# Natural keys taken from the products of A, 40-column stationaries, a scheduler that counts instruction transfers, and 128-row products for y

## The chip, the cores and the metric

The kernel runs on one core of a Trainium2 chip. The metric is the device time of one execution in microseconds (us); less is better. The engines are TensorE (PE, with its weight loader PEld), VectorE (DVE), ScalarE (ACT), GpSimd (POOL) and SyncE (SP, which here only issues DMAs).

## The reference, cut to what matters

A recurrence over 768 steps for 4 x 8 heads of 40 x 40 state, and a gated feed-forward block on its output:

```python
for t in range(S):
    y[:, :, t] = einsum('bhd,bhde->bhe', rt, state)
    Sa = einsum('bhde,bhe->bhd', state, at)
    state = state * wt[:, :, None, :] - einsum('bhd,bhe->bhde', Sa, bt)
    state = state + einsum('bhd,bhe->bhde', vt, kt)
xn = x / sqrt(mean(x * x) + 1e-6) * rms_g      # x: 3072 x 320
g = xn @ w_gate;  val = xn @ w_val             # 320 x 1536, stored as float64
out = (g * sigmoid(g) * val) @ w_out           # 1536 x 320
```

## The kernel before, in words

**Tiling.** The recurrence is cut into 24 chunks of C = 32 steps; all 32 heads are worked at once, as 8 groups n of (i, o) pairs: i is the upper or lower 64 partitions where the steps of k and b (or v and U) lie, o which head of the pair. LEVELS = 1, 2, 4, 8, 16 are the steps of a doubling scheme inside a chunk.

**`front(c)`** (L467) needs only the inputs. It loads w and a (`wan`), k and b (`kbn`), v (`VU`) and every second w (`wn`), turns them on PE (`turned`, 8 transposes of 128x128 against `ident`), and then for each level l multiplies K and A (32 products, "A,K", L502), puts the result under a mask into LT (`where`, DVE), and scales K and A for the next level (DVE and ACT copies). `natural` (L456) turns K back so that its steps lie on partitions (`KN[l]`): 8 transposes and a copy, for l = 4, 8, 16 and 32, so four K transposes a chunk. LT goes through DRAM (`sB`) into M, one row of 32 x 32 per head.

**`inverse(c)`** (L537) solves M by 31 pairs of small DVE operations on `Yi` and sends the result back through `sY` into LT.

**`main(c)`** (L558) is the recurrence over chunks: X (ST,aP and VU,LT), U (Xs,LT), the state update "up" (VU,KN), the scores sc (rE,vut), their masked copies As (one per level, DVE, L609), y's base (rE,Sd and r,Sd, L638) and five `level` products (As,KN, L616: 32 products of 64 rows x 64 stationary columns, 16 moving columns). Of the 64 stationary columns 24 are not needed (the next head's, or padding). Then y is turned (`xn`), squared on ACT (`sq`, with a sum), raised to -1/2 on POOL, scaled on ACT to x, turned again ("ident,x", L666) and scaled to `xg`.

**`feed(g)`** (L671) works on two chunks: for 12 blocks f of 128 columns of the feed-forward, 4 products on 128 rows and 2 on 64 rows (inputs 256 to 319) in one batch (L685), Silu (ACT), a product (DVE) and 2 output products (L690). Weights come from `sW` in DRAM into five buffers `wf`. `narrow` (L701), 24 calls, first converts them from float64 there, through the buffers wf, sg and hT that the feed uses too.

**What sets the order.** Nothing is issued when it is written. `plan.add` takes each piece with an engine, a due time and a cost; `Plan.issue` (L118) then runs a simulation and writes the program in the order that comes out. Each engine takes, of the pieces that are ready, the one due first. For PE it also models a clock that halves after a 3.41 us window with few columns (ENOUGH, KEEP, L47) and prefers wide pieces then, and it puts fillers (`warm`, L740: a 128x128 product that nobody reads) into PE's idle time until the first feed product. SP's and ACT's DMA issues are pieces too; `swapped` (L451) issues k, b and v on ACT's queue, all other loads are on SP's.

Of the kernel before, what the change touches and what calls it, by code (L numbers as in the profile page):

```python
# [22 lines left out]
N0, NF = 60.0, 6.0  # L23
S0, S1 = 36.0, 8.0
LAG = 10.0
EPS = 1e-6


class Piece:


    def __init__(self, engine, due, time, issue, lane=0.0, columns=0, paced=False, room=None, since=0.0):
        self.engine, self.due, self.time, self.issue = engine, due, time, issue
        self.lane, self.columns, self.paced, self.room = lane, columns, paced, room
        self.ready, self.missing, self.users = since, 0, []


class Plan:
# [6 lines left out]
    LATENCY, SELF = 0.18, 0.115  # L45
    SWITCH, STICK = 0.1, 4.0
    WINDOW, ENOUGH, KEEP = 3.41, 1600, 1300  # L47
    LOOK, LOW = 1.0, 1300
    AHEAD, FAR = 0.0, 20.0
    WARM = 200.0  # L50
# [67 lines left out]
    def issue(self):  # L118
# [5 lines left out]
        clock, columns, recent, lane, order, full, fed = [0.5], {}, [], 0.0, [], False, False  # L124

        def put(i):
            p = P_[i]
            (held if p.paced and p.due > pace + self.FAR else waiting[p.engine]).append(i)

# [7 lines left out]
        for _ in P_:  # L137
            t, e = min((max(free[e], min(at_least(i) for i in w)), e) for e, w in waiting.items() if w)
            can = [i for i in waiting[e] if at_least(i) <= t]
            if e == "PE":  # L140
                since = max(free[e], 3.0)
                while not fed and t < self.WARM and since + 0.3 < t:
                    w = int(since / self.WINDOW)
                    while len(clock) <= w:
                        c = columns.get(len(clock) - 1, 0)
                        clock.append(1.0 if c >= (self.ENOUGH if clock[-1] < 1 else self.KEEP) else 0.5)
                    order.append((since, None))
                    columns[w] = columns.get(w, 0) + 256
                    since += 0.214 / clock[w]
                at = int(t / self.WINDOW)  # L150
                while len(clock) <= at:
                    c = columns.get(len(clock) - 1, 0)
                    clock.append(1.0 if c >= (self.ENOUGH if clock[-1] < 1 else self.KEEP) else 0.5)
# [3 lines left out]
                many = [i for i in can if P_[i].columns >= 500]  # L157
                if many and (clock[at] < 1 or had < self.LOW):
# [3 lines left out]
            i = min(can, key=lambda i: (P_[i].due + (self.STICK if e == "PE" and (P_[i].columns > 0) != full else 0), i))  # L162
# [3 lines left out]
            if e == "PE":  # L166
                end = t + (p.time + (self.SWITCH if (p.columns > 0) != full else 0)) / clock[at]
                full, fed = p.columns > 0, fed or p.paced is True
# [5 lines left out]
            if p.lane:  # L174
                lane = max(lane, end + 1.2) + p.lane
                end = lane + 0.7
# [9 lines left out]
            for j in p.users:  # L186
                u = P_[j]
                u.ready = max(u.ready, end + (self.LATENCY if u.engine != e else 0 if e == "PE" else self.SELF))
                u.missing -= 1
                if not u.missing:  # L190
                    put(j)
# [19 lines left out]
def kernel(  # L211
# [122 lines left out]
    def mm(o, lhsT, rhs, start=True, stop=True):  # L334
        return o, lhsT, rhs, lambda at: nc.tensor.matmul(at(o), lhsT, rhs, start=start, stop=stop, skip_group_check=True)  # L335

    def flip(o, i, ident):
        return o, i, ident, lambda at: nc.tensor.transpose(at(o), i, ident)  # L338

    def pe(due, time, steps, columns=0, paced=False, more=[]):  # L340
        def issue(at):
            for s in steps:
                s[3](at)
        plan.add("PE", due, time + 0.02, issue, [s[0] for s in steps] + more, [x for s in steps for x in s[1:3]],
                 columns=columns, paced=paced)
# [5 lines left out]
                            compare_op=ALU.not_equal, fill=1.0)  # L351

# [6 lines left out]
    for j, l in enumerate(LEVELS):  # L359
        nc.vector.tensor_scalar(iw[:, 2], iw[:, 0], j, None, ALU.logical_shift_right)  # L360
        nc.vector.tensor_scalar(msk[:, j], iw[:, 2], 1.0, None, ALU.is_equal)
    mhalf = const.tile([P, 1], FP32, name="mhalf")
# [31 lines left out]
    tail = lambda t: t[:, NI * D:]  # L394
# [4 lines left out]
    VU_ = Turns(2, [P, N, 2, 64], "VU", whole)  # L399
    ST_ = Turns(2, [P, N, 2, 64], "ST", whole)  # L400
    LT_ = Turns(3, [P, NI, C], "LT", whole)
    KN_ = {l: Turns(3, [P, NI * D + 24], f"KN{l}_", tail) for l in LEVELS[1:] + (32,)}
    Sd_ = Turns(2, [P, NI * D + 24], "Sd", whole)
    T_ = Turns(3, [P, NI * 63], "T")
    K_ = Turns(3, [P, NI, 2, C], "K")
    A_ = Turns(3, [P, NI, C], "A")
    aP_ = Turns(2, [P, NI, C], "aP")
    M_ = Turns(1, [P, C, C], "M")
# [7 lines left out]
    As_ = Turns(1, [P, len(LEVELS), NI, 16], "As")  # L416
# [11 lines left out]
    po_ = psum.tile([P, 2, 512], FP32, name="po")  # L428
# [13 lines left out]
    def turned(due, t, paced=False):  # L442

        ps = plan.room().rearrange("p u f -> p (u f)").rearrange("p (n t) -> p n t", n=N)
        pe(due, 0.95, [flip(ps[:, n, :], t[:, n].rearrange("p o e -> p (o e)"), ident) for n in range(N)], 1024, paced)
# [5 lines left out]
    def swapped(due, t, i, x, src, tk):  # L451

        for q in range(2):
            dma(due, flat(t)[rows(i, x ^ q), q * H:(q + 1) * H, 0:D], src[2 * i + q, :, tk, :].rearrange("h s d -> s h d"), "ACT")

    def natural(due, l, K):  # L456
        ps = turned(due, K.rearrange("p (n i) x s -> p n i (x s)", i=2))
        t = KN_[l].next()
        copy(due, t[:, 0:NI * D].rearrange("p (n o e) -> p n o e", n=N, o=2),
             ps.rearrange("p n (o e) -> p n o e", o=2)[:, :, :, 0:D])  # L460
        return t

    def kn(z, l, i, n, o):
        w_ = D if l > 1 else 64
        return z["KN"][l][half(i), (2 * n + o) * w_:(2 * n + o) * w_ + 64]

    def front(c):  # L467
# [5 lines left out]
        for i in range(2):  # L473
# [6 lines left out]
            for x in range(2):  # L480
                at = i * 64 + x * C
                dma(d - T, wn[at:at + C:2], w[2 * i:2 * i + 2, :, c * C + 1:(c + 1) * C:2, :].rearrange("q h s d -> s (q h) d"))
        ps = turned(d + 4.2, wa).rearrange("p n (i x t) -> p (n i) x t", i=2, x=2)
# [6 lines left out]
        copy(d + 7.2, Tl[1], ps[:, :, 0, :])  # L490
        A = A_.next()
        copy(d - 0.9, A, ps[:, :, 1, :])
        K = K_.next()
        copy(d + 2, K.rearrange("p (n i) x s -> p n (i x s)", n=N), turned(d + 2, kb))
        LT = z["LT"] = LT_.next()
        z["KN"] = {1: flat(kb).rearrange("p a e -> p (a e)"), 2: KN_[2].next()}
        tt(d + 1.3, z["KN"][2][:, 0:NI * D].rearrange("p (a e) -> p a e", e=D), flat(kb)[:, :, 0:D], wn, MUL)
        for j, l in enumerate(LEVELS):
            G = C // (2 * l)
            due = d + 5 + 7.5 * j  # L500
            gr = plan.room().rearrange("p o (n t) -> p o n t", n=N)[:, :, :, 0:16]
            pe(due - 0.7, 0.95, [mm(gr[half(i), o, n, :], K[part(o), 2 * n + i].rearrange("p x s -> p (x s)"),  # L502
                              side(A, l, 1)[part(o), 2 * n + i]) for n, i, o in each])
            where(due, side(LT, l, 1), side(msk, l, 1)[:, j:j + 1].bitcast(U32).to_broadcast((P, NI, G, l)),
                  gr.rearrange("p o n t -> p (o n) t").rearrange("p n (g l) -> p n g l", g=G))
            if l > 2:
                z["KN"][l] = natural(due + 2, l, K)
# [4 lines left out]
            if G == 1 or l == 1:  # L512
                lr = lambda t: t.rearrange("p n x (g h l) -> p n x h (g l)", h=2, l=l)
                tt(due + 0.1, lr(K1)[:, :, :, 0], lr(K)[:, :, :, 0], t[:, :, None, :, 1].to_broadcast((P, NI, 2, 16)), MUL)
            else:
                for x in range(2):
                    tt(due + 1.6, side(K1[:, :, x], l, 0), side(K[:, :, x], l, 0), by[1], MUL)
            for x in range(2):
                copy(due, side(K1[:, :, x], l, 1), side(K[:, :, x], l, 1))
            A1 = A_.next() if l < 16 else aP_.next()  # L520
            tt(due - 7.7, side(A1, l, 1), side(A, l, 1), by[0], MUL)
            copy(due, side(A1, l, 0), side(A, l, 0))
            tt(due - 3, Tl[2 * l], t[:, :, :, 0], t[:, :, :, 1], MUL)
# [4 lines left out]
        for i, q in each_iq:  # L528
            for o in range(2):
                dma(due - 2.1, sB[seq(i, q, o)].rearrange("m (s t) -> s m t", s=C), LT[rows(i, 1 - q), o * N + 4 * q:o * N + 4 * q + 4])  # L530
        z["M"] = M = M_.next()
        for m in range(4):
            dma(due, M[m * BH:(m + 1) * BH].rearrange("p s t -> p (s t)"), sB)
        z["KN"][32] = natural(due + 7.8, 32, K)
        z["aP"] = A

    def inverse(c):  # L537
# [5 lines left out]
        pcopy(d + 2.1, Y, eye)  # L543
        for i in range(C - 1):
            n, m = i // 4 + 1, C - 1 - i
            tmp = tmp_.next()[:, 0:n * m].rearrange("p (s t) -> p s t", s=n)
            tt(d + i - 1.1, tmp, Y[:, 0:n, i:i + 1].to_broadcast((P, n, m)), M[:, i:i + 1, i + 1:].to_broadcast((P, n, m)), MUL)
            tt(d + i + 7.2, Y[:, 0:n, i + 1:], Y[:, 0:n, i + 1:], tmp, SUB)
        sY = sY_.next()
        for m in range(4):  # L550
            dma(d + C - 0.8, sY.rearrange("n (j m t) -> m n j t", m=4, t=C)[m], Y[m * BH:(m + 1) * BH])
        for i, q in each_iq:
            for o in range(2):
                dma(d + C - 0.5, LT[rows(i, 1 - q), o * N + 4 * q:o * N + 4 * q + 4], sY[seq(i, q, o)].rearrange("m (s t) -> s m t", s=C))
# [3 lines left out]
    def main(c):  # L558
# [5 lines left out]
        pe(d - 10.3, 0.65, [mm(X[other(i, n), o, col(n % 4)], z["aP"][part(o), 2 * n + i], ST[part(o), n, i, 0:D], n % 4 == 0, False)  # L564
                     for n, i, o in each], paced=None)
        pe(d - 20.2, 0.6, [mm(X[other(i, n), o, col(n % 4)], LT[own(i, n), o * N + n], VU[own(i, n), n, o, 0:D], False, n % 4 == 3)
                    for n, i, o in by_q], paced=None)
        Sdec = Sdec_.next()
        tt(d - 0.5, Sdec, ST.rearrange("p n i d -> p (n i) d")[:, :, 0:D], z["T"][32].to_broadcast((P, NI, D)), MUL)
        Xs = Xs_.next()  # L570
        scale(d + 0.2, Xs, X[:, :, 0:4 * D], -1.0)
# [3 lines left out]
        for i, q in each_iq:  # L575
            (copy, dcopy)[q](d + 8, VU[other(i, 4 * q), 4 * q:4 * q + 4, :, 0:D].rearrange("p n o d -> p o n d"),
# [196 lines left out]
```

## Time and profile before

| what | value |
|---|---|
| three runs | 1407.22, 1406.03 and 1397.87 us, median 1406.03 |
| the profiled execution's own time | 1420.57 us |
| its span, first to last instruction | 1418.8 us |
| mean granted clock of TensorE | 0.929 |
| matmul passes | 29810 |
| instruction DMAs (queue q8) | 234, 3.83 MB |
| HBM | 125.83 MB read, 16.12 MB written, 100 GB/s |
| DMA packets | 307935, 37.2% of the 16 engines' time on SP's queue, 5.4% on ACT's |

An fp32 product is two passes in the trace, a transpose one, so 32 products are a batch of x64. In a row of the time line the first number is the start, the second the time from there to the end of the last pass; batches overlap, so the cost of one is the distance to the next one's start. "[4.30 <-ACT x]" is idle time ahead of a row and what ended it; "issue" is idle time for which the profile shows no wait. Names are given without buffer numbers: ps is any of three PSUM pairs.

### The profile page before, as it was taken

The numbers are of one execution on the slowest core, as the hardware profiler recorded it, in microseconds if no ns is written. First come the engines' busy times: TensorE is split into PE (matmuls) and PEld (weight loads), VectorE is DVE, ScalarE is ACT, GpSimd is POOL, SyncE is SP. The second block draws the span as 40 slices with busy tenths as digits, with TensorE's granted clock in tenths as the row PEclk, the third lists the DMA queues.
The fourth block names the chain that finished last, engine by engine and source line by source line (L and its number), as shares of the span: only waits on it lengthen the run. The fifth ranks groups of instructions, "written<-read, shape, count | busy, mean of one in ns | idle before, by whom it ended". The sixth has DMA issues, their size and how long they took to land.

```text
span 1418.8 us, 66685 instructions
## 1 busy us (share of the span) xinstructions
PE 1271.6 (90%) x29810; PEld 1031.6 (73%) x29810; DVE 834.8 (59%) x2939; ACT 457.4 (32%) x985; POOL 43.7 (3%) x118
## 2 busy tenths in 40 slices
PE   7997878989899889899898898998898989999998
PEld 7886767778677668677676676776776777777775
DVE  4777878547547457366375475574574665674420
ACT  2633544322423324224223233233233233242111
POOL 3000000000000000000000000000000000000000
PEclk8997667999999999899998999999999999999999
DMA  5465465444444435335434345434443444533332
GB/s 85 104 166 135 122 144 130 119 87 113 101 101 108 87 72 125 78 98 110 91 91 88 90 107 101 106 88 94 100 106 80 110 98 95 115 94 96 92 117 84
DMA packets 307935, 146.31 MB, mean 103 GB/s; under 512 B 270784, under 2 KB 284608, under 8 KB 307648
## 3 DMA queue, kind: packets, MB, share of 16 engines
q1 hardware_dynamic: 229312, 130.23, 37.2%
q10 hardware_dynamic: 78336, 11.81, 5.4%
q8 instruction: 234, 3.83, 1.1%
q14 instruction: 53, 0.43, 0.1%
HBM read 125.83 MB, written 16.12 MB: 100 GB/s over the span
## 4 chain that ended last, share of the span: by engine, by line
PE 55%; issue 14%; DVE 14%; DMA 8%; SPq 4%; ACT 3%; POOL 2%; ACTq 0%; POOLq 0%; DVEq 0%
PE ps L335 36%; PE ps L338 10%; PE po L335 9%; DMA sY<-Yi 4%; SPq L332 4%; DVE tmp L291 3%; DVE Yi L291 3%; DVE hT L291 2%; DVE y L291 1%; DVE K L291 1%; DVE LT L291 1%; POOL ss L321 1%; DMA LT<-sY 1%; ACT sg L311 1%; DVE sg L291 1%
## 5 line engine op out<-in xcount | busy, mean ns | idle before, releaser
L335 PE MATMUL ps<-xg,wf 128*128 128x256 f32 (+1 forms) x1728 | 405.6, 426 | 4.5 <-DVE hT L291 2.5
L335 PEld LDWEIGHTS ps<-xg,wf 128*128 128x128 f32 (+1 forms) x1728 | 275.4, 203 | 97.4 <-issue 56.2
L311 ACT ACTIVATE sg<-ps 128x256 f32<-128x256 f32 x144 | 55.2, 383 | 501.3 <-PE ps L335 328.0
L335 PE MATMUL po<-wf,hT 128*128 128x320 f32 x576 | 195.3, 463 | 0.0
L291 DVE TENSOR_TENSOR hT<-ps,sg 128x256 f32<-128x256 f32 x144 | 60.9, 423 | 196.7 <-ACT sg L311 195.9
L291 DVE TENSOR_TENSOR tmp<-Yi,M 128x60 f32<-128x60 f32 (+24 forms) x744 | 156.0, 210 | 20.1 <-DMA M<-sB 4.4
L291 DVE TENSOR_TENSOR Yi<-Yi,tmp 128x60 f32<-128x60 f32 (+24 forms) x744 | 155.6, 209 | 15.6
L335 PEld LDWEIGHTS ps<-A,K 40*64 40x64 f32 x7680 | 131.5, 140 | 39.1 <-issue 32.3
L335 PE MATMUL ps<-A,K 40*64 40x16 f32 x7680 | 144.3, 211 | 15.0 <-issue 10.5
L335 PEld LDWEIGHTS po<-wf,hT 128*128 128x128 f32 x576 | 100.0, 193 | 32.5 <-issue 6.2
L335 PE MATMUL ps<-As,KN 64*64 64x16 f32 x6144 | 116.0, 212 | 6.1 <-issue 6.0
L335 PEld LDWEIGHTS ps<-As,KN 64*64 64x64 f32 x6144 | 107.5, 143 | 16.0 <-issue 14.0
L315 ACT COPY KN<-ps 128x640 f32<-128x640 f32 x96 | 66.2, 690 | 155.7 <-PE ps L338 126.5
L338 PE MATMUL ps<-ident,K 128*128 128x128 f32 x768 | 109.1, 289 | 3.0 <-DVE Yi L291 1.1
L338 PEld LDWEIGHTS ps<-ident,K 128*128 128x128 f32 x768 | 95.0, 150 | 22.5 <-issue 4.5
L291 DVE TENSOR_TENSOR y<-y,ps 128x256 f32<-128x256 f32 (+1 forms) x192 | 59.2, 319 | 85.9 <-PE ps L335 84.2
L291 DVE TENSOR_TENSOR K<-K,T 128x512 f32<-128x512 f32 (+1 forms) x192 | 92.3, 486 | 6.8 <-ACT K L315 6.5
L315 ACT COPY K<-K 128x256 f32<-128x256 f32 x240 | 90.4, 414 | 16.9 <-DMA VU<-in_v_dram 7.6
L291 DVE COPY_PREDICATED LT<-msk,ps 128x256 f32<-128x256 uint32 x120 | 66.2, 551 | 45.6 <-PE ps L335 44.1
L291 DVE TENSOR_TENSOR A<-A,T 128x256 f32<-128x256 f32 x96 | 40.3, 419 | 62.4 <-ACT T L315 62.3
L338 PE MATMUL ps<-ident,x 128*128 128x128 f32 x72 | 17.8, 367 | 64.6 <-ACT x L318 64.6
L740 PE MATMUL po<-ident 128*128 128x128 f32 x466 | 67.9, 309 | 1.5 <-POOL ident L350 1.4
(95 smaller groups left out, 1352.3 us busy)
## 6 DMA issues: line engine op xcount, KB each, us to landing
wf<-sW SPq DMA_DIRECT2D x144, 480.0 KB, 3.8
M<-sB SPq DMA_DIRECT2D x96, 128.0 KB, 4.4
sW<-hT SPq DMA_DIRECT2D x24, 240.0 KB, 3.7
kbn<-in_k_dram ACTq DMA_DIRECT2D x96, 40.0 KB, 2.8
wan<-in_w_dram SPq DMA_DIRECT2D x48, 80.0 KB, 3.0
kbn<-in_b_dram ACTq DMA_DIRECT2D x96, 40.0 KB, 2.6
wan<-in_a_dram SPq DMA_DIRECT2D x48, 80.0 KB, 2.6
wn<-in_w_dram SPq DMA_DIRECT2D x96, 40.0 KB, 2.3
```

Of the source, the lines that this page charges most:

```text
L291: plan.add("DVE", due, time + 0.00104 * size(o), lambda at: fn(at(o), *m(at)), [o], aps(*args))
L311: plan.add("ACT", due, 0.08 + 0.00083 * size(o), lambda at: nc.scalar.activation(at(o), at(a), f, **kw), [o] + aps(acc), [a])
L315: plan.add("ACT", due, 0.08 + 0.00083 * size(o), lambda at: nc.scalar.copy(at(o), at(a)), [o], [a])
L321: plan.add("POOL", due, 0.12 + 0.0021 * size(o), lambda at: nc.gpsimd.tensor_tensor(o, a, b, op), [o], [a, b])
L332: plan.add(by, due, 0.45, lambda at: queue.dma_start(out=o, in_=i), [o], [i], lane=max(0.4, n * 4 / 220e3), since=since)
L335: return o, lhsT, rhs, lambda at: nc.tensor.matmul(at(o), lhsT, rhs, start=start, stop=stop, skip_group_check=True)
L338: return o, i, ident, lambda at: nc.tensor.transpose(at(o), i, ident)
L740: plan.warm = lambda: nc.tensor.matmul(po_[:, 0, 0:P], ident, ident, start=True, stop=True)
```

## The change

- **Natural keys.** The tiles of A for levels 4, 8 and 16 (`Ab`) carry 40 further columns that hold the identity, and their right halves stand in columns 16 to 31. So the A,K batch streams 56 columns (16 of A, 40 of identity) for 16, and KN[4], KN[8] and KN[16] are copied from its result. `natural` is gone; only KN[32] is still turned. A's scaling and copying for these levels is done in two halves.
- **40-column stationaries.** "up" and y's base use 40 stationary columns, not 64; the padding of KN and Sd goes.
- **y with 128 rows.** As is written twice as wide, with a zero block for the other half (mask `msi`), so that a `level` is 16 products of 128 rows x 40 stationary columns with 32 moving ones. y's sum takes one DVE operation a level.
- **The feed** goes in pairs of blocks: first the 64-row products of both, then each block's four 128-row products as a batch of its own.
- **The scheduler** counts instructions (256 to a transfer, one at most every 3.6 us) and charges a piece that would stall; fillers go on until 230 us of its time (`WARM`), also ahead of ready work when the columns run low (`FILL`); other constants and most due times change. `warm` writes a part of `po` that is set to zero once.
- **Loads.** From chunk 3 on k, b and v are issued by SP. The weights' loads may start at 15 + 5f us of the scheduler's time, not 36 + 8f, and their conversion is due at -10 + 6f, not 60 + 6f.
- **Buffers.** K and A two for three, Ab two, M two for one.

```diff
-N0, NF = 60.0, 6.0
-S0, S1 = 36.0, 8.0
+N0, NF = -10.0, 6.0
+S0, S1 = 15.0, 5.0
+M40 = 0.75
+EARLY = 3
...
+    LINE, FETCH, STALL = 256, 3.6, 5.0
...
+                def run(p):
+                    time = (p.time + (self.SWITCH if p.tiled == full else 0)) / clock[at]
+                    end, left, done, begun, lost = t, p.many, line[0], line[1], 0.0
+                    while done + left >= self.LINE:
+                        n = self.LINE - done
+                        end += time * n / p.many
+                        lost += max(0.0, begun + self.FETCH - end)
+                        end = begun = max(end, begun + self.FETCH)
+                        left, done = left - n, 0
+                    return end + time * left / p.many, (done + left, begun), lost
+                runs = {i: run(P_[i]) for i in can}
+                i = min(can, key=lambda i: (P_[i].due + (self.STICK if P_[i].tiled == full else 0) + self.STALL * runs[i][2], i))
...
-            dma(due, flat(t)[rows(i, x ^ q), q * H:(q + 1) * H, 0:D], src[...], "ACT")
+            dma(due, flat(t)[rows(i, x ^ q), q * H:(q + 1) * H, 0:D], src[...], "ACT" if tk.start < EARLY * C else "SP")
...
+            wide = 16 if l <= 2 else 16 + D
+            pe(due - 14.5, 0.95, [mm(gr[half(i), o, n, 0:wide], K[part(o), 2 * n + i].rearrange("p x s -> p (x s)"),
+                              side(A, l, 1)[part(o), 2 * n + i] if l <= 2 else A[part(o), 2 * n + i, 16:]) for n, i, o in each],
+               10 * wide, tiled=True)
...
             if l > 2:
-                z["KN"][l] = natural(due + 2, l, K)
+                z["KN"][l] = KN_[l].next()
+                copy(due + 2, z["KN"][l].rearrange("p (n o e) -> p n o e", n=N, o=2), gr.rearrange("p o n t -> p n o t")[:, :, :, 16:wide])
...
         def level(due, ps, j):
-            pe(due, 0.95, [mm(ps[half(o), i, n], kn(z, LEVELS[j], i, n, o), As[half(i), j, o * N + n]) for n, i, o in each], paced=None)
+            pe(due, M40, [mm(ps[part(o), n], z["KN"][LEVELS[j]][:, kn_at(LEVELS[j], n, o)],
+                              As[:, j, o * N + n].rearrange("p i t -> p (i t)")) for n in range(N) for o in range(2)],
+               320, None, tiled=True)
```

Where the program moves. First PE in the middle of the run, behind y's base of one chunk (po is the feed's output product, xg,wf its input products, As a level of y, ident,y the turning of y). Before:

```order
L335 MATMUL po<-wf_189,hT_196 128x320 x2
L338 MATMUL ps_75<-ident,K_161 128x128 x8
L335 MATMUL ps_76<-xg_188,wf_191 128x256 x6
L335 MATMUL ps_77<-A_165,K_161 64x16 x32
L335 MATMUL ps_75<-As_179,KN_0_144 64x16 x32
L335 MATMUL po<-wf_190,hT_197 128x320 x2
L338 MATMUL ps_76<-ident,K_162 128x128 x8
L335 MATMUL ps_75<-As_179,KN_0_141 64x16 x32
L335 MATMUL ps_75<-As_179,kbn_129 64x16 x32
```

Now:

```order
L368 MATMUL po<-wf_209,hT_214 128x320 x2
L368 MATMUL ps_76<-xg_205,wf_210 128x256 x4
L368 MATMUL ps_77<-As_197,KN_2_163 40x32 x16
L368 MATMUL ps_77<-As_197,KN_2_160 40x32 x16
L368 MATMUL ps_77<-As_197,kbn_148 40x32 x16
L371 MATMUL ps_75<-ident,K_179 128x128 x8
L368 MATMUL po<-wf_210,hT_215 128x320 x2
L368 MATMUL ps_77<-ident,y_198 64x40 x16
```

Two K transposes are gone from this stretch and the levels follow each other with 16 products each; the one K transpose left is that of KN[32].

Second ScalarE between y's base and x, in the middle of the run. Before:

```order
L311 ACTIVATE sg_195<-ps_75 128x256
L315 COPY KN_0_150<-ps_75 128x640
L332 DMA kbn_130<-in_k_dram 32x8x40 x2
L332 DMA kbn_130<-in_b_dram 32x8x40 x2
L332 DMA kbn_130<-in_k_dram 32x8x40 x2
L332 DMA kbn_130<-in_b_dram 32x8x40 x2
L311 ACTIVATE sg_194<-ps_76 128x256
L311 ACTIVATE sq_184,ss_182<-ps_77 128x320
L318 ACTIVATE x_185<-ps_77,ss_182 128x2x4x40
```

Now:

```order
L348 COPY y_198<-ps_75 128x2x8x16
L344 ACTIVATE sg_213<-ps_77 128x256
L348 COPY KN_0_170<-ps_75 128x640
L344 ACTIVATE sq_202,ss_200<-ps_76 128x320
L348 COPY T_176<-ps_75 128x512
L351 ACTIVATE x_203<-ps_76,ss_200 128x2x4x40
```

The eight loads of k and b ahead of the square are gone from this queue; SP issues them among its copies from sY to LT.

Third PE at the start, ahead of chunk 0's first product (ST,aP). Before:

```order
L338 MATMUL ps_77<-ident,K_163 128x128 x8
L740 MATMUL po<-ident 128x128 x127
L335 MATMUL ps_76<-ST_136,aP_167 32x40 x32
L335 MATMUL ps_76<-VU_134,LT_138 32x40 x32
L740 MATMUL po<-ident 128x128 x3
```

Now:

```order
L371 MATMUL ps_75<-ident,K_179 128x128 x8
L812 MATMUL po<-ident 128x128 x192
L368 MATMUL ps_77<-ST_153,aP_184 32x40 x32
L368 MATMUL ps_77<-VU_151,LT_155 32x40 x32
L812 MATMUL po<-ident 128x128 x4
```

The block of fillers grows from 127 to 192; over all, 202 fillers stand ahead of chunk 0 before and 314 now, 233 and 349 in the whole program. The first feed product stood behind the levels of chunk 2 and stands behind those of chunk 1 now.

More of the change, by code (lines that the diff above doesn't have):

```diff
@@ L141, in issue @@
                 since = max(free[e], 3.0)
[L142 to L153, printed above, removed]
+                while t < self.WARM and since + 0.3 < t:
+                    since = fill(since)
+                t = max(t, since)
                 since = t + self.LOOK - self.WINDOW
@@ L166, in issue @@
             if e == "PE":
-                end = t + (p.time + (self.SWITCH if (p.columns > 0) != full else 0)) / clock[at]
-                full, fed = p.columns > 0, fed or p.paced is True
+                end, line, _ = runs[i]
+                full = not p.tiled
                 over = min(1.0, max(0.0, (end - (at + 1) * self.WINDOW) / (end - t)))
```

303 lines of the change are left out of this document (175 added, 128 removed).

## The prediction

> **What bounds the kernel now.** I read the page first, then the stages, then who waits for whom, then single stretches in order of time. On the page:
>
> ```profile
> PE 1271.6 (90%) x29810; PEld 1031.6 (73%) x29810; DVE 834.8 (59%) x2939; ACT 457.4 (32%) x985; POOL 43.7 (3%) x118
> ...
> PEclk8997667999999999899998999999999999999999
> ```
>
> TensorE is busy nine tenths of the span and no other engine reaches two thirds of that. Its clock is low in a stretch near the start and never quite full after it. The first feed-forward product on PE starts at 234.11 us (row below), so I cut there (columns: stretch; length, then busy us of PE, PEld, DVE, ACT, POOL; clock; DMA share; GB/s):
>
> ```profile
> 0.00:234.10 234.10, 190.76 (x4488) 178.34 (x4488) 171.32 (x540) 106.85 (x209) 18.09 (x55) 0.79 0.54 128
> 234.10:1418.80 1184.70, 1080.86 (x25323) 853.29 (x25322) 663.52 (x2399) 350.54 (x776) 25.64 (x63) 0.96 0.42 98
> ```
>
> After the cut PE is idle 1184.7 - 1080.9 = 104 us, and a mean clock of 0.96 means that 4% of the stretch, 47 us, is lost to the slow clock: 151 us of losses; the rest is work. So two things can shorten the stretch: fewer or shorter products, and fewer losses. The losses, as PE's waits in that stretch:
>
> ```profile
> PE ps L338 <- ACT x L318: 58.2, 17, 5.0
> PE ps L335 <- issue: 25.1, 28, 2.7
> ```
>
> 58 of 104 us are one wait: the transposes of x stand at the head of PE's queue and ScalarE has not written x. One of the 17:
>
> ```profile
> 745.37 1.04 PE L338 MATMUL ps<-ident,K 128*128 128x128 f32 x8
> 750.70 0.90 PE L338 MATMUL ps<-ident,x 128*128 128x128 f32 x3 [4.30 <-ACT x L318]
> 751.39 4.55 PE L335 MATMUL ps<-xg,wf 128*128 128x256 f32 x12
> ```
>
> PE stands still 4.30 us, and then the next batch takes 4.55 us where the same batch takes 2.56 (below): a window with little work is answered by half clock. ScalarE in the same microseconds:
>
> ```profile
> 739.73 0.83 ACTq L332 DMA_DIRECT2D kbn<-in_k_dram  x2
> ...
> 747.32 0.98 ACTq L332 DMA_DIRECT2D kbn<-in_b_dram  x2
> 748.40 0.38 ACT L311 ACTIVATE sg<-ps 128x256 f32<-128x256 f32 x1 [9.49 <-DMA LT<-sY]
> 748.68 0.43 ACT L311 ACTIVATE sq<-ps 128x320 f32<-128x320 f32 x1
> ```
>
> ScalarE computes nothing for 9.49 us while it issues eight copies of k and b; the square that x needs is queued behind them. The cause is ScalarE's own DMA issues, not its arithmetic (32% busy).
>
> **The change part by part: PE's work.** What a batch costs is the distance to the start of the next one, in a stretch at full clock:
>
> ```profile
> 1255.58 1.14 PE L335 MATMUL ps<-VU,KN 64*64 64x40 f32 x64
> 1256.65 1.34 PE L335 MATMUL po<-wf,hT 128*128 128x320 f32 x4
> ...
> 1259.00 1.12 PE L335 MATMUL ps<-A,K 40*64 40x16 f32 x64
> 1259.96 1.11 PE L335 MATMUL ps<-rE,vut 40*64 40x32 f32 x64
> 1261.00 2.63 PE L335 MATMUL ps<-xg,wf 128*128 128x256 f32 x12
> 1263.56 1.09 PE L338 MATMUL ps<-ident,K 128*128 128x128 f32 x8
> 1264.58 1.12 PE L335 MATMUL ps<-A,K 40*64 40x16 f32 x64
> 1265.54 1.10 PE L335 MATMUL ps<-As,KN 64*64 64x16 f32 x64
> 1266.57 1.34 PE L335 MATMUL po<-wf,hT 128*128 128x320 f32 x4
> ...
> 1292.74 0.79 PE L335 MATMUL ps<-ST,aP 40*32 40x40 f32 x64
> 1293.47 0.79 PE L335 MATMUL ps<-VU,LT 32*32 32x40 f32 x64
> ```
>
> So a transpose of K is 1.02 us, products with 16 moving columns 0.96, with 32 1.04, with 40 1.07, a level of y 1.03, and a batch with 32-column stationaries 0.73.
>
> - Natural keys: of four K transposes a chunk three go, 72 batches at 1.0: -72 us. Their work lies in a row with PE's other batches, with nothing beside it, so it counts in full.
> - In their place 72 batches of A,K products get 56 moving columns for 16. From 16 to 40 the rows rise by 0.11; carried on to 56 that is +0.18, taken as +0.15: +11 us. Bounds: 0 (the weight loads hide it) and +40 (half as long again).
> - Levels of y, five a chunk, 120 batches: 64 passes become 32, each over 128 rows with 40 stationary columns. Each column half of the array still gets 16 passes of each column group, and the rows say that stationary columns set the pace (32: 0.73, 64: 1.03); 40 lies at 0.80. So 120 x 0.23 = -28. Bounds: 0 (the pass sets the pace and the columns nothing) and -61 (half the passes, half of 1.03).
> - The state update and the base of y go from 64 to 40 stationary columns: 24 x (1.07 - 0.80) + 24 x (0.96 - 0.80) = -10. Bounds 0 and -14.
> - The feed's products on 64 rows now run once for two blocks. The weight loader's row:
>
> ```profile
> L335 PEld LDWEIGHTS ps<-xg,wf 64*128 64x128 f32 x576 | 46.0, 195 | 52.5 <-issue 52.5
> ```
>
> 52.5 us idle before 144 such stretches; with 72 half would go, -26 at most. Part of it is overlapped by the matmul still running: -10. Bounds -26 and 0.
>
> Sum of work -109 us; with every end together -32 to -173.
>
> The Trainium skill, "TensorEngine Tiling (Array Packing)", section "Instruction Overhead", says that a matmul of free dimension 1 has the same latency as one of 60; by it the 56-column products would be free and the work sum would be -120. The rows rise by 0.11 us between 16 and 40 columns, so the trace agrees only roughly, and I stay with +11.
>
> **Off PE.** VectorE writes the weights of y with their zero blocks: per chunk six of 256 and two of 512 elements where five of 256 stood.
>
> ```profile
> L291 DVE TENSOR_TENSOR As<-ps,msk 128x256 f32<-128x256 f32 x120 | 45.4, 417 | 3.6 <-PE ps L335 3.6
> ...
> L291 DVE TENSOR_TENSOR K<-K,T 128x512 f32<-128x512 f32 x48 | 32.9, 686 | 5.7 <-ACT K L315 5.4 <-PE ps L338 0.2
> ```
>
> 6 x 0.417 + 2 x 0.686 - 5 x 0.417 = +1.8 us a chunk, some 40 us in all. The other edits on VectorE and ScalarE (A's copies halved in size and doubled in number, y added in one piece) move under half a microsecond a chunk each. Beside 663 us busy in 1184.7 this is covered by PE's own queue; if the cover went, 40 us would come back.
>
> **The start.** Rows of PE's time line, and of the stores of the converted weights:
>
> ```profile
> 71.80 28.53 PE L740 MATMUL po<-ident 128*128 128x128 f32 x254
> 100.25 0.79 PE L335 MATMUL ps<-ST,aP 40*32 40x40 f32 x64
> ...
> 234.11 3.92 PE L335 MATMUL ps<-xg,wf 128*128 128x256 f32 x12
> ```
>
> ```profile
> L332 SPq DMA_DIRECT2D sW<-hT x24: 315/377/1375, 74.6 to 236.0; - x24
> ```
>
> The feed starts when the weights are done. The change starts their conversion earlier, and in the new order the first feed product stands behind chunk 1's levels, not chunk 2's. Fillers ahead of chunk 0 go from 202 to 314; a filler is two passes of 28.53 / 254, so +25 us, less nine dropped transposes: chunk 0 starts near 110 (100 to 116). From there to the feed the order holds some 45 us of batches and fillers; with waits of 25 us as they are today it starts at 180 (160 to 225). By the batch prices above, 95 us of real work stand ahead of the feed today and 64 then, so 31 us more are left behind it: (180 - 234) + 31 = -23. Bounds -43 and +22.
>
> **The waits.** From chunk 3 on k, b and v are issued by SP, which computes nothing, and ScalarE's square follows its copies at once: of 58 us I keep 10, -48. The new order counts PE's instruction transfers; of 25 us "issue" I keep 12, -13. The half clock follows both kinds of stall: of 47 us I keep 25, -22. What is late next: with some 8 us less per chunk VectorE goes from 56% to some 67% and SP gets 12 more issues a chunk, so I add 18 us of new waits. Sum -65; bounds -120 (30 us of losses left) and +20.
>
> **Sum.** -109 - 23 - 65 = -197 us, against the profiled execution's span of 1418.8 us (its own time 1420.57): 1222 us of span. The median of the runs, 1406.03, is 14.5 below that execution's time, so the forecast for the time is 1406 - 197 = **1209 us**.
>
> **The rivals.**
>
> 1. The waits stay. ScalarE's hold may come from the copies themselves and not from who issues them: its row names a copy of SP's (LT<-sY) as the end of the wait. Then x waits for something else as long, the losses stay 151 us, and only -109 - 23 is left: **1274**. Against it: the ACT rows show issue instructions in the gap, and on SP no arithmetic stands behind them. The Trainium skill, "DMA: Bandwidth & Descriptors", section "Issuing engines are not separate DMA queues", says that issuing from several engines saves only the sequencer's time, "usually small relative to the DMA itself"; by that rule the move gains little and this rival holds. Here the hold is 9.49 us, which is not small, so the trace speaks against it.
> 2. Losses nearly gone: 30 us left of 151, -109 - 23 - 121: **1153**. For it: nearly all waits that PE has now are of two kinds, and the change meets both. Against: a shorter chunk brings every other engine nearer.
> 3. Slower: SP becomes the bound.
>
> ```profile
> 742.67 4.74 SPq L332 DMA_DIRECT2D LT<-sY  x8
> 747.51 3.70 SPq L332 DMA_DIRECT2D sB<-LT  x8
> ```
>
> ```profile
> SPq L332 <- PE po L335: 297.0, 64, 10.3
> ```
>
> By the loops SP issues 43 copies a chunk, at (4.74 + 3.70) / 16 = 0.53 us 23 us; a chunk lasts (1292.74 - 100.25) / 22 = 54.2 us. If k and b hold SP for 9.5 us as they hold ScalarE, v for half that, SP needs 37 us; if also its waits for free weight buffers (297 us, 14 a chunk) and as much as 5 us for its own chains stay in the row, 56 us. Above 54.2 it decides: +1.8 x 22 = 40 us slower and no gain: **1446**. Against it: the waits for buffers are slack that shrinks when PE is faster.
> 4. Nothing comes out: what is taken from PE lies beside a chain through VectorE that sets the pace. **1406**. Against it: VectorE is 56% busy and hardly appears in PE's waits.
>
> **How the numbers follow.** Forecast 0.68, rival 1 0.14, rival 2 0.10, rival 3 0.05, rival 4 0.03. A difference of 1% is about what a measurement of this kernel can tell from none. Faster by over 1%: 0.68 + 0.14 + 0.10 = 0.92; within 1%: 0.03; slower: 0.05. The range takes in rivals 1 and 2 and leaves out the joint ends of the work bounds: 1140 to 1290 us.
>
> **What would show it.** Right: K transposes x192 in the trace for x768; a level of y at 0.7 to 0.9 us; 56-column batches at 1.0 to 1.3; PE's wait for ACT x under 20 us; a first feed product between 160 and 225 us; PE still the busiest engine at 85 to 92%, clock 0.95 or more after the feed's start. Wrong: PE under 80% busy with waits for LT, U or wf (then rival 3 or 4); x waits as long as now (rival 1); a feed that starts after 230; levels at 1.0.

## The result and the profile after

The changed kernel takes 1271.64 us (median of 4 runs, 1260.05 to 1282.96) where the kernel before took 1406.62 beside it: ratio 0.9025, interval 0.8939 to 0.9112. It is faster by 135 us; 197 were forecast. The profiled executions of both kernels are slow ones, about 1% above their medians, so they are compared with each other here (span 1281.1 for 1418.8, -138); the experiments are compared with a second profile of the changed kernel, of 1265.0.

The page of the changed kernel: PE's busy share stays, VectorE's is up.

```profile
PE 1152.5 (90%) x25626; PEld 937.6 (73%) x25626; DVE 887.6 (69%) x3012; ACT 467.3 (36%) x1060; POOL 47.3 (4%) x118
...
PEclk9999668999898899999999997989999998999999
```

Cut again at the first feed-forward product, now 204.22 us (columns as before: stretch; length, busy us of PE, PEld, DVE, ACT, POOL; clock; DMA share; GB/s):

```profile
0.00:204.20 204.20, 167.91 (x3472) 158.48 (x3472) 161.66 (x498) 102.39 (x209) 19.95 (x54) 0.86 0.64 145
204.20:1281.10 1076.90, 984.59 (x22158) 779.15 (x22154) 725.90 (x2514) 364.87 (x851) 27.36 (x64) 0.95 0.45 108
```

Behind the cut PE is idle 1076.9 - 984.6 = 92 us for 104 before, and the clock is no better (0.95 for 0.96). So PE has less work, and the losses stayed. PE's longest waits in the whole run:

```profile
PE po L368 <- DVE hT L324: 21.9, 23, 2.4
PE ps L368 <- issue: 21.6, 24, 3.7
PE ps L368 <- DVE y L324: 13.0, 19, 3.2
PE ps L368 <- DVE hT L324: 9.3, 12, 1.9
PE ps L368 <- ACT K L348: 8.4, 6, 3.9
```

The wait for x, 64.6 us in the whole run before, is 0.9 now; waits for VectorE (hT, y) have come in its place. The batches, in a stretch at full clock and then two levels of y at once:

```profile
830.27 1.16 PE L368 MATMUL ps<-Ab,K 40*64 40x56 f32 x64
831.36 1.14 PE L368 MATMUL ps<-xg,wf 64*128 64x256 f32 x8
832.42 0.83 PE L368 MATMUL ps<-VU,KN 64*40 64x40 f32 x64
833.18 1.99 PE L368 MATMUL ps<-xg,wf 128*128 128x256 f32 x8
835.01 1.05 PE L371 MATMUL ps<-ident,VU 128*128 128x128 f32 x8
```

```profile
897.82 1.42 PE L368 MATMUL ps<-As,KN 128*40 128x32 f32 x64
899.16 1.14 PE L368 MATMUL ps<-xg,wf 64*128 64x256 f32 x8
```

From start to start: a 56-column batch 1.09, the state update 0.76 (1.07 before), a level (899.16 - 897.82) / 2 = 0.67 (1.03 before).

To see where 138 us came from I cut the time of PE in both traces into idle time, time lost to half clock (half of the time that the clock records show at half speed, whether PE was busy or idle), fillers, and what is left as work at full clock:

| us | before | after | difference |
|---|---|---|---|
| real work | 1114 | 989 | -125 |
| fillers | 57 | 84 | +27 |
| idle and half clock ahead of the cut | 43 + 48 | 36 + 30 | -26 |
| idle and half clock behind it | 104 + 53 | 92 + 50 | -14 |

Idle moments at half clock stand in two rows here, and so too little is left as work. With half clock counted only while PE is busy (41 and 48 us before, 25 and 48 after), work is 1127 us before and 996 after, -130.

### The profile page after: what moved, and what is told of

Read it like the earlier page. It is cut to its first block, busy times and chain, and to the rows that moved or that the text cites. A ratio compares the mean times of both kernels' runs of the same rounds, so it can differ in the third digit from the quotient of the medians.

```text
span 1281.1 us, 58318 instructions
## 1 busy us (share of the span) xinstructions
PE 1152.5 (90%) x25626; PEld 937.6 (73%) x25626; DVE 887.6 (69%) x3012; ACT 467.3 (36%) x1060; POOL 47.3 (4%) x118
## 4 chain that ended last, share of the span: by engine, by line
PE 44%; DVE 26%; SPq 12%; DMA 9%; issue 5%; ACT 3%; POOL 0%; DVEq 0%; POOLq 0%; ACTq 0%
PE ps L368 29%; SPq L365 12%; PE po L368 8%; DVE tmp L324 5%; DVE Yi L324 5%; PE ps L371 4%; PE po L812 4%; DMA M<-sB 3%; DVE As L324 3%; DVE hT L324 2%; DVE K L324 2%; DVE LT L324 2%; DVE y L324 2%; DMA sW<-hT 1%; DMA kbn<-in_k_dram 1%
## 5 line engine op out<-in xcount | busy, mean ns | idle before, releaser
L368 PEld LDWEIGHTS ps<-Ab,K 40*64 40x64 f32 x4608 | 80.2, 143 | 36.1 <-issue 19.3
L368 PE MATMUL ps<-Ab,K 40*64 40x56 f32 x4608 | 90.5, 229 | 13.1 <-ACT K L348 6.2
L812 PE MATMUL po<-ident 128*128 128x128 f32 x698 | 93.7, 293 | 6.6 <-POOL eye L421 5.2
L812 PEld LDWEIGHTS po<-ident 128*128 128x128 f32 x698 | 88.1, 206 | 7.9 <-POOL eye L421 5.2
L324 DVE TENSOR_TENSOR As<-ps,msi 128x512 f32<-128x512 f32 (+1 forms) x192 | 80.1, 484 | 7.3 <-PE ps L368 7.3
L368 PEld LDWEIGHTS ps<-As,KN 128*40 128x40 f32 x3072 | 67.5, 128 | 22.8 <-issue 7.1
L368 PE MATMUL ps<-As,KN 128*40 128x32 f32 x3072 | 73.8, 208 | 6.7 <-DVE hT L324 5.8
L368 PEld LDWEIGHTS ps<-A,K 40*64 40x64 f32 x3072 | 54.5, 145 | 26.1 <-issue 15.8
L368 PE MATMUL ps<-A,K 40*64 40x16 f32 x3072 | 59.7, 214 | 7.1 <-issue 3.1
L324 DVE TENSOR_TENSOR y<-y,ps 128x256 f32<-128x256 f32 x120 | 50.6, 421 | 19.8 <-PE ps L368 17.4
```

The costliest lines, as they stand in the source:

```text
L324: plan.add("DVE", due, time + 0.00104 * size(o), lambda at: fn(at(o), *m(at)), [o], aps(*args))
L812: plan.warm = lambda: nc.tensor.matmul(po_[:, 0, DM:DM + P], ident, ident, start=False, stop=False, skip_group_check=True)
```

## The experiments

Theory A, at first, for the losses that stayed: with 12 more issues a chunk SP brings M late, VectorE's inverse waits for M, hT stands behind the inverse in VectorE's queue, and PE waits for hT. The changed kernel shows it (SP, DVE and PE rows of one stretch):

```profile
324.60 0.81 PE L368 MATMUL ps<-As,kbn 128*40 128x32 f32 x32 [0.52 <-DVE y L324]
325.83 0.94 SPq L365 DMA_DIRECT2D M<-sB  x2
...
326.81 0.93 SPq L365 DMA_DIRECT2D kbn<-in_k_dram  x2
327.78 2.11 SPq L365 DMA_DIRECT2D kbn<-in_b_dram  x2
329.94 0.94 SPq L365 DMA_DIRECT2D kbn<-in_k_dram  x2
330.93 0.94 SPq L365 DMA_DIRECT2D kbn<-in_b_dram  x2
331.91 0.56 SPq L365 DMA_DIRECT2D sY<-Yi  x1
...
332.51 1.06 SPq L365 DMA_DIRECT2D M<-sB  x2
...
333.49 1.04 PE L371 MATMUL ps<-ident,kbn 128*128 128x128 f32 x8
...
336.06 0.19 DVE L324 TENSOR_TENSOR tmp<-Yi,M 128x31 f32<-128x31 f32 x1 [0.77 <-DMA M<-sB]
...
339.51 2.19 PE L368 MATMUL po<-wf,hT 128*128 128x320 f32 x4 [2.20 <-DVE hT L324]
...
343.46 3.57 PE L368 MATMUL ps<-xg,wf 128*128 128x256 f32 x8
```

Eight loads of k and b part the four copies of M, and 2.20 us of waiting are followed by a batch at half clock (3.57 us; 1.99 in the rows at full clock above). Its rivals: B, VectorE simply has too much arithmetic; C, the dense work that the change removed had covered other engines' latencies and kept the clock up. "Order untouched" below means that the planner decides as in the kernel it stands beside, and only what is issued differs. The table gives PE's idle time and half-clock loss behind the cut, and waits in the whole trace; PE's work behind the cut is 929 to 936 us in all variants of the changed kernel except where the work was put back (1046) and where the feed starts later (907). The last five rows are newly planned orders. The rows were measured in three sets; the kernel before took 1403 us beside the first four, 1416 beside "planned anew", "loads due later", "fourth buffer" and "old conversion", and 1407 beside the others, so between sets the ratio is to be compared and not the time.

| kernel | us | ratio, interval | idle | half clock | PE for hT | PE for x | DVE for M |
|---|---|---|---|---|---|---|---|
| changed, again | 1269.9 | 0.906 (0.899-0.913) | 92 | 38 | 35 | 2.5 | 21.7 |
| k,b,v on ScalarE | 1320.8 | 0.943 (0.938-0.949) | 131 | 49 | 30 | 50.8 | 0.9 |
| k,b,v not loaded | 1235.7 | 0.882 (0.876-0.888) | 79 | 22 | 24 | 1.2 | 4.2 |
| half of As | 1263.5 | 0.903 (0.897-0.910) | 85 | 34 | 25 | 1.4 | 24.7 |
| k,b,v on GpSimd | 1277.2 | 0.908 (0.900-0.915) | 101 | 44 | 22 | 12.4 | 2.0 |
| work put back | 1331.2 | 0.946 (0.938-0.954) | 54 | 15 | 13 | 0 | 8.7 |
| planned anew | 1267.1 | 0.892 (0.887-0.898) | 89 | 32 | 26 | 0 | 18.0 |
| loads due later | 1283.1 | 0.904 (0.898-0.909) | 102 | 43 | 28 | 3.5 | 27.6 |
| fourth buffer | 1237.2 | 0.873 (0.868-0.877) | 79 | 20 | 27 | 0.9 | 7.0 |
| fourth buffer, later | 1229.1 | 0.873 (0.865-0.882) | 73 | 13 | 33 | 0.7 | 17.1 |
| old conversion | 1270.1 | 0.897 (0.892-0.902) | 83 | 29 | 29 | 3.1 | 29.7 |

**The yardstick.**

> The changed kernel once more, as the yardstick for the kernels that run beside it on the same chip: 1272 us, between 1260 and 1283, 0.90 of the kernel before.

**Who issues k, b and v.** In the changed kernel:

```diff
-    ..., "ACT" if tk.start < EARLY * C else "SP")
+    ..., "ACT" if tk.start < EARLY * C else "SP", to="ACT")
```

(the planner books the first name, the engine in `to` issues.)

> The changed kernel with its order untouched, but k, b and v of chunk 3 onward issued by ScalarE at the place of the order that SP had. Theory A (the 12 more issues a chunk hold SP up, M comes late, the inverse's first step on VectorE waits, and hT stands behind it): the waits for hT (31 us) and VectorE's wait for M (23 us) fall by half or more, the waits for x come back with 40 to 60 us, so 1275 to 1310 us. Theory B (VectorE has too much arithmetic): waits for hT stay and the waits for x come on top, 1310 to 1340 us. If ScalarE's own issues never were the cause of the waits for x: these stay under 10 us and the time at 1272.

1320.8 us, +51. The wait for x is back:

```profile
PE ps L371 <- ACT x L351: 50.8, 17, 5.5
PE po L368 <- DVE hT L324: 18.5, 15, 2.7
```

So ScalarE's own issues are what delays x, and moving them is worth 51 us in this order. The time lies in the range that theory B had asked for; that theory is tried below.

But VectorE's wait for M falls to 0.9 us and PE waits for hT as long as before (30 us for 35): the last link of theory A does not hold in this kernel. The same move in the kernel before:

```diff
-    ..., "ACT")
+    ..., "ACT", to="SP" if tk.start >= 3 * C else None)
```

> The kernel before with its order untouched, but k, b and v of chunk 3 onward issued by SP at the place of the order that ScalarE had. If ScalarE's own issues cause the waits for x (65 us in the whole run), these fall under 15 us and about as much is saved as the reverse move cost in the changed kernel (51 us), less some waits for M: 1345 to 1375 us. If ScalarE's arithmetic or PE's order causes them, they stay over 40 us: 1395 us or more. If SP is then too late for M and LT: waits for M, LT or hT over 25 us in their place, 1380 to 1410 us.

1442.2 us beside 1407: ratio 1.026 (1.017 to 1.035), slower. No reading came out whole: the second's size (1395 or more) without its sign, waits for x over 40 us, and the third's mechanism above its size (1380 to 1410). The wait for x is gone (0.9 us), and what replaces it is dearer; VectorE's and PE's largest:

```profile
DVE tmp L291 <- DMA M<-sB: 99.7, 22, 6.8
```

```profile
PE ps L338 <- DVE tmp L291: 49.8, 11, 6.6
PE ps L335 <- DVE hT L291: 33.0, 8, 5.3
```

One of them, SP, DVE and PE in order of time:

```profile
577.72 1.10 PE L335 MATMUL ps<-As,kbn 64*64 64x16 f32 x64
578.38 0.83 SPq L332 DMA_DIRECT2D kbn<-in_k_dram  x2
579.27 1.76 SPq L332 DMA_DIRECT2D kbn<-in_b_dram  x2
...
597.50 3.16 SPq L332 DMA_DIRECT2D M<-sB  x4
...
603.93 0.19 DVE L291 TENSOR_TENSOR tmp<-Yi,M 128x31 f32<-128x31 f32 x1 [5.67 <-DMA M<-sB]
604.81 0.82 DVE L291 TENSOR_TENSOR ST<-ps,Sdec 128x640 f32<-128x640 f32 x1
...
605.77 1.94 PE L338 MATMUL ps<-ident,ST 128*128 128x128 f32 x8 [5.48 <-DVE tmp L291]
607.64 1.91 PE L335 MATMUL ps<-A,K 40*64 40x16 f32 x64
609.37 1.91 PE L335 MATMUL ps<-rE,vut 40*64 40x32 f32 x64
```

M is issued late on SP, VectorE stands 5.67 us in front of it with the state update ST behind, PE stands 5.48 us for ST, and three batches run at half clock (1.9 us for 1.1). Theory A's chain is real: with waits of up to 6.8 us it is paid by PE (half clock lost behind the cut goes from 53 to 88 us), with waits of at most 2.4 (the changed kernel) it mostly isn't. The planner had booked these issues on ScalarE; the move pays only together with an order that knows of it.

**What the issues cost SP.** First without the loads (later chunks compute on old data), then with GpSimd as issuer:

```diff
+    go = (lambda at: None) if skip else (lambda at: queue.dma_start(out=o, in_=i))
```

> The changed kernel with its order untouched, but k, b and v are loaded for the first three chunks only; later chunks work on old data (work left out). Theory A: the waits for hT, for M and their half clock go, 30 to 60 us, so 1210 to 1240 us. Theory B: SP and the transfers were not it, 1260 to 1275 us, waits for hT near 31 us.

```diff
+    ..., to="POOL" if tk.start >= EARLY * C else None)
```

> The changed kernel with its order untouched, but k, b and v of chunk 3 onward issued by GpSimd. Theory A: neither ScalarE nor SP is held up, so waits for x stay under 8 us and VectorE's wait for M falls under 8 us: 1238 to 1258 us. Rival: GpSimd's issues hold up its own work, the power that x needs and the copies of eye, or the loads land later, so that waits for x, K or Yi take the place: 1275 to 1310 us.

Without them 1235.7 us, -34 and in theory A's range, two thirds of it in half clock and time ahead of the cut; but the waits for hT fall only from 35 to 24 us. Copies of M land after 2.6 us for 2.7 (medians), so the loads do not slow M's own transfer. With GpSimd issuing them, SP relieved just as well and VectorE's wait for M down to 2.0 us, nothing is gained: 1277.2, as the rival had it. There PE waits 12 us for x from GpSimd and ScalarE, and "issue" waits rise from 20 to 36 us; the transfers change as well (8064 packets for k, b and v, where SP's make 68544). So SP's time and M in time bring no gain by themselves here; how much of one the new waits hide, this run does not tell. What the loads themselves do to PE had to be looked at.

**VectorE's load.** Of As only the first block is written from chunk 1 on (the second instruction is planned and not issued; where one instruction writes both blocks, not shown here, it writes half):

```diff
-    for i in range(2): tt(d + 18, As[:, j, :, i], ...)
+    for i in range(2): tt(d + 18, As[:, j, :, i], ..., (None, ()) if c and i else None)
```

> The changed kernel with its order and every product untouched, but from the second chunk on VectorE writes only the first of the two blocks of As (the other keeps old data, work left out): about 37 us less on VectorE. Theory A: hT still stands behind an inverse that waits for M, 1255 to 1275 us. Theory B: hT and y come earlier, their 40 us of waits and the half clock behind them shrink by half or more, 1205 to 1240 us. Theory C (with the dense transposes gone the columns in a window lie near the gate's threshold, so that any small stall costs several windows): 1240 to 1265 us, with the half clock (27 us lost now) falling more than the waits.

1263.5, not to be told from 1269.9. Theory B, which asked for 1240 at most, falls: 31 us less arithmetic behind the cut (694 us busy for 725) leave the waits for y where they were and take 10 us off those for hT. The time is in the ranges of theories A and C both.

**PE's work put back.** Eight fillers behind each of the 72 wide batches:

```diff
+            for _ in range(behind):
+                plan.warm()
```

> The changed kernel with its order untouched and eight idle 128x128 products on PE behind each of the 72 batches with 56 moving columns: as many passes as the 72 batches of transposes that the change removed, by 0.12 us each 69 us of work, dense for the clock. Theory W (each microsecond of PE's work counts in full): 1330 to 1345 us, idle time and half clock as before. Theory C (removing them uncovered waits for other engines and let windows fall below the gate's threshold): waits for hT, y and M (45 us) and half clock (about 40 us lost) fall by a third or more, 1285 to 1315 us.

The price in that text is half of the true one: a filler is two passes. PE's group of them has 1850 passes where the changed kernel has 698:

```profile
L814 PE MATMUL po<-ident 128*128 128x128 f32 x1850 | 240.0, 286 | 5.2 <-POOL eye L423 5.2
```

By the cut in four the added fillers are 140 us at full clock, not 69. The time rises by 61 (57 by the ratios). So 1331.2 lies in the range on record for theory W only because that was reckoned with half the work: with the true price it asks for some 1410, and idle time and half clock did not stay. Theory W falls, and theory C holds: behind the cut 114 us of work were added and idle time and half clock fell from 92 + 38 to 54 + 15, 61 us. PE's waits for hT fall from 35 to 13 us, VectorE's for M from 21.7 to 8.7; those for y stay. Dense work beside them hides the other engines' chains; that the batches removed had done so follows as far as the fillers stand for them.

**When k and b come.** In the rows from 324 us above, SP can load k and b only once the level of y that read this buffer three chunks back is done (324.60; in the median the first load goes 1.2 us after it), and PE's transposition of them starts 1.6 us after the last issue (333.49). Over all chunks the median from the last issue to the transposition is 3.4 us; before it was 6.8. A fourth buffer takes this away (room comes from the third buffer of the keys of level 32); the due time of the loads of k (here) and b was tried with it and without:

```diff
-    kbn = Turns(3, [P, N, 2, 64], "kbn", pad)
+    kbn = Turns(4, [P, N, 2, 64], "kbn", pad)
-    KN_ = {l: Turns(3, [P, NI * D], f"KN{l}_") for l in LEVELS[1:] + (32,)}
+    KN_ = {l: Turns(2 if l == 32 else 3, [P, NI * D], f"KN{l}_") for l in LEVELS[1:] + (32,)}
-            swapped(d - T, kb, i, 0, k, tk)
+            swapped(d - T + (16 if c >= EARLY else 0), kb, i, 0, k, tk)
```

> The changed kernel with a fourth buffer for k and b (room for it comes from the third buffer of the keys of level 32) and the loads of k and b due 16 us later; planned anew. Now these loads need not wait for the last level of y three chunks back, and M goes ahead of them on SP. Theory A (12 issues beside M make M and with it VectorE late): VectorE's wait for M falls from 22 us to under 8, waits for hT and half clock fall, 1235 to 1255 us. Rival (M's lateness on VectorE is idle time that costs PE nothing; the gain of leaving the loads out came from something else): 1262 us or more.

> The other half: a fourth buffer for k and b (the third of the keys of level 32 given up), loads due as in the changed kernel. If the loads' wait for the last level of y three chunks back, and PE's transposes behind it, make the 41 us: 1225 to 1245 us with less half clock (under 60 us of it behind the feed's start). If the due time does: 1262 us or more.

> Of the kernel with four buffers for k and b the later due time alone: three buffers as in the changed kernel, loads of k and b due 16 us later, so that M goes ahead of them on SP. If the place of M on SP makes the 41 us: 1235 to 1250 us with VectorE's wait for M under 8 us. If the buffer does: 1262 us or more.

> The changed kernel planned anew with the feed-forward's due times 0.3 us later and nothing else: how much a new order alone is worth. 1255 to 1285 us if orders of this planner are worth about the same; outside that, no difference of another order below its size can be put down to an edit.

Both edits give 1229.1 us, the buffer alone 1237.2, the due time alone 1283.1, and a new plan without an edit 1267.1. The new plans without the fourth buffer (old conversion among them) lie at ratios of 0.892 to 0.904, the two with it at 0.873 each, ahead of both kernels that the study began with. So the buffer makes the gain, 30 us beside the new plan of the same set, and the later due time adds nothing that can be told. M's place on SP does not make it: the later due time was meant to put M first, but by itself VectorE's wait for M grew to 27.6 us, and with both edits VectorE waits 17.1 us for M, about as in the new plan without an edit (18.0; theory A had asked for under 8), at 0.873 for 0.892. With both:

```profile
600.77 0.81 PE L368 MATMUL ps<-As,kbn 128*40 128x32 f32 x32 [0.52 <-DVE y L324]
...
603.63 2.60 SPq L365 DMA_DIRECT2D M<-sB  x4
...
607.20 1.04 PE L371 MATMUL ps<-ident,kbn 128*128 128x128 f32 x8
...
612.67 0.92 SPq L365 DMA_DIRECT2D kbn<-in_k_dram  x2
```

```profile
213.00:1227.20 1014.20, 941.51 (x22042) 756.32 (x22034) 708.92 (x2480) 360.38 (x842) 28.65 (x64) 0.99 0.48 114
```

The transposition at 607.20 uses loads issued one chunk earlier (some 34 us in the median), those at 612.67 are for the next. Clock 0.99 and 73 us idle behind the cut, for 0.96 and 92 in the yardstick. Whether the early data itself or the freer order of the planner does it, these runs do not part.

**The start.**

```diff
-N0, NF = -10.0, 6.0
-S0, S1 = 15.0, 5.0
+N0, NF = 60.0, 6.0
+S0, S1 = 36.0, 8.0
...
-            dma(d - T, rw[p0:p0 + s.shape[0], o:o + s.shape[1]], ...
+            dma(d - T - 12.6, rw[p0:p0 + s.shape[0], o:o + s.shape[1]], ...
```

> The changed kernel with the weights' conversion at its old due times, planned anew. If the earlier conversion is worth the 23 us that the prediction gave the start: the first feed-forward product near 230 us and 1288 to 1300 us in all. If the feed only starts sooner and takes with it work that else stands ahead of it: 1260 to 1278 us, with as much more work ahead of the cut as the cut comes later.

1270.1 us, no difference from the 1267.1 of the new plan in the same set; the feed starts at 249.8:

```profile
0.00:249.80 249.80, 219.40 (x4897) 204.73 (x4897) 200.82 (x663) 122.06 (x255) 22.11 (x58) 0.91 0.58 129
249.80:1269.30 1019.50, 936.52 (x20947) 742.12 (x20937) 687.42 (x2350) 344.98 (x805) 25.28 (x60) 0.97 0.47 111
```

Ahead of the cut stand 46 us more, behind it 42 us less than in the yardstick. With half clock counted while PE is busy, the 46 us are 26 us of work and 28 us of fillers more, and 8 us less idle time and half clock; the 42 us are 25 us of work, 2 of fillers and 15 of idle time and half clock. So the second reading has the time right, but only about half of the delay is work that goes first; the rest is made good by smaller losses in an order that is new as a whole. When the feed starts decides nothing by itself.

## Why the prediction was right, and where it was not

Right in direction, and the 1272 us lie inside 1140 to 1290; the forecast of 1209 was too low by 63. The work on PE, which makes nearly all of the gain, came out as reasoned; two of the other terms did not. By its terms, with work, start and waits as in the first of the two counts above:

| term | foretold | measured |
|---|---|---|
| K transposes | -72 | -63 (87.6 to 24.3 us of PE's time) |
| 56 columns for 16 | +11 | +2 (128.6 to 130.9) |
| levels of y | -28 | -35 (118.3 to 83.4) |
| state update, base of y | -10 | -14 (50.3 to 36.6) |
| feed's 64-row products | -10 | -14 (353.7 to 339.3 for all of its input products) |
| work in all | -109 | -125 (-130 in the second count) |
| start | -23 | +1 (27 us more fillers, 26 us less idle time and half clock) |
| waits and half clock behind it | -65 | -14 |

**The work** was sized well, each product by its own row (the single terms are in the second count; with some -6 us of small ones they make up its -130). The levels are cheaper than the rule "stationary columns set the pace" made them (0.67 to 0.74 us, 0.80 taken): with 64 passes and 40 stationary columns the state update takes 0.76, so the halved passes also count. Idle time ahead of the 64-row products' weight loads halved, as foretold (52.5 to 26.3 us). The Trainium skill, "TensorEngine Tiling (Array Packing)", section "Instruction Overhead", would have had the 56 columns for nothing; +2 in all agrees with it better than my +11.

**The start failed as a term.** Chunk 0 starts at 117 us (110 foretold) and the feed at 204 (180). For chunk 0 the prediction's own figures, 100.25 + 25 - 9, make 116, not 110. From there to the feed (columns as above):

```profile
117.22:204.22 87.00, 62.45 (x1805) 56.62 (x1804) 75.74 (x229) 45.76 (x93) 2.65 (x5) 0.72 0.62 152
```

PE is idle for 25 us, as foretold, and batches and fillers at full clock take 43 us where 45 were reckoned. The step that failed is the sum "some 45 us of batches and fillers; with waits of 25 us", which puts the half clock at nothing: it took 20 us while PE was busy, at a mean clock of 0.72. With the 7 us of chunk 0, less 2 of batches, that makes the feed 24 us late, and the 23 are gone. The run with the old conversion says more: the feed may start 46 us later at no cost.

**The waits failed.** "ScalarE's square follows its copies at once" was right (x waits 0.9 us, 10 were kept), and moving the issues is worth 51 us, measured by moving them back. The step that failed is "I add 18 us of new waits": what came instead was 31 us for hT (2.5 before) and 13 for y (none), and 22 us "issue" where 12 were kept. PE's idle time behind the cut is 92 us where the sum leaves 104 - 48 - 13 + 18 = 61, and half clock 50 where 25 were kept (of 53 by the clock records; the rounded 0.96 gave 47). In the second profile they are 92 and 38. So the half clock did not go down with the wait for x as far as the sum had it. The sum had no term for what work taken from PE uncovers: of the transposes it said that their work "counts in full". Where 140 us of other dense products were put back, only some 60 were lost; that the transposes themselves had this rate is inferred from it, not measured. What PE still waits for once k and b come early, hT and y with some 45 us and "issue" with 18, no run here took away, and why the waits for hT came stays open beyond that they shrink with more work on PE.

The time lies at rival 1's 1274 by chance, not by its mechanism: x no longer waits. A rule that spoke for it, in the Trainium skill, "DMA: Bandwidth & Descriptors", section "Issuing engines are not separate DMA queues", holds that the sequencer's time which issuing on several engines saves is usually small relative to the DMA itself; here who issues is worth 51 us in one order and costs 35 in another, by what stands behind the issues. Rival 3, SP as the bound, did not come (PE is 90% busy), yet its mechanism is what the kernel before shows with the new queue. Rival 4 fell.

## What to carry to other kernels

Work taken from a busy engine may not come back in full where other engines' chains were hidden beside it: put work back and see what it costs before counting it as gain. What a late item in a queue costs depends on what stands behind it, so moving issues to another queue is one edit with the order that knows of it. A load that is issued just as its buffer comes free and used a few microseconds later is worth a trial with one more buffer, even where no wait in the profile names it; here that was worth 30 us, by the early data or by the order that it allowed.

## What the runs showed of the hardware

- Two levels of y, each of 16 products of 128 rows x 40 stationary and 32 moving columns, take 1.34 us, 21 ns a pass, where 64-row, 64-column stationaries took 1.03 us for 64 passes, 16 ns a pass.
- GpSimd takes 0.59 us for an issue of k (49.1 us for 84), SP some 0.47 (0.94 for two in the rows above). With GpSimd as issuer PE waits 6.3 us for GpSimd's copy of x and 6.1 for ScalarE's x; the power that x needs stands in GpSimd's queue too.
- With 114 us more of dense products behind the cut PE was idle 38 us less and ran 46 us less at half clock (75 to 29).
